# Attention and a Fourier mix on one core: score tiles in a fixed uneven order of two cycles, and the Fourier targets added on GpSimd

## The chip, the cores and the metric

The kernel runs on one core of one Trainium2 chip. A core has a matrix engine (TensorE; PE in the profile, with PEld for its weight loads), VectorE (DVE), ScalarE (ACT), GpSimd (POOL) and SyncE (SP), which only issues DMAs here. The metric is the device time of one execution in microseconds (us), lower is better.

## The reference

The input is x, 2048 tokens of 640 numbers. Two branches are computed from it and mixed by a gate per token:

```
g = sigmoid((x * gate_w).sum(-1))
a = softmax(q k^T / sqrt(20)) v, 32 heads of 20, then @ wo        # attention
b = Cr @ (x @ Hr) - Ci @ (x @ Hi)                                 # Fourier mix
out = g * a + (1 - g) * b
```

Cr, Ci are the 2048x2048 cosine and sine matrices along the sequence, Hr, Hi the 640x640 ones along the hidden axis. All inputs are given as arguments and all arithmetic is float32.

## The kernel before

**Precision.** Where float32 accuracy is wanted from the faster `fp32r` matmul, an operand is split in two (`split`, L90: a rounded copy and the remainder) and three products are added.

**Scores.** Two heads lie in the two halves of the partitions (rows 0 to 63 and 64 to 127), so a score matmul (60 or 62 rows, 128x512 results, one PSUM bank) uses one half of the array, and two on different halves run side by side. A softmax needs the row maximum first, so each score tile is computed twice. A *maximum tile* (`s_mm`, L151) is a 128x512 matmul whose maximum over 512 columns VectorE takes (L153). 41 steps (`LEAD`) later the *exponential tile* (L638) computes the same scores transposed, with minus the maximum as two more rows of the operand, and ScalarE writes the exponentials into a tile `p` (L641). A unit is a pair of heads and half of the queries: 32 steps, each of two exponential and two maximum tiles. There are 32 units (`NU`), 1024 steps. After a unit's last maximum tile, VectorE reduces the maxima once more (L159), PE transposes them (`max_chain`, L179) and SP stores them as rows of `qst`.

**Banks.** All score tiles, and that transpose, take the five banks `ps0` to `ps4` in turn (`bank`, L104). So a score matmul has to wait until the tile five places earlier has been read by its reader, ScalarE or VectorE. PE executes in program order: an instruction that waits holds back everything behind it.

**Cycles.** Four steps make a cycle. At its end comes the burst: `av_step` (L429) multiplies the exponentials of eight finished tiles by v, 16 matmuls on L435, into the bank `av`. So a cycle has eight exponential tiles, eight maximum tiles and one burst, 256 cycles in all.

**Fillers.** Between score tiles PE gets pieces of the Fourier branch, called fills here: a fill is two 320-column matmuls, one on each half of the array. In the first 54 cycles they come from `hid_tile` (L287, x times the hidden DFT, 15 fills a cycle, one tile each cycle); after three cycles without, they come from `dft_step` (L510), 48 for each of 56 units of the sequence DFT. A DFT unit is spread over three cycles (16 fills each, 26 units) or four (12 fills each, 30 units). In a cycle they stand in seven slots, after each pair of score tiles but the last (`goals`, `fill`). A step's order on PE is: exponential, maximum, fills, exponential, maximum, fills.

**The targets.** The sequence DFT is done with sums and differences of its blocks (`PRODUCTS`), so that each product is added to one or two targets, tiles of y. At a unit's end ScalarE and VectorE read its two banks into `m` (L529, L530), and `finish_y` (L537) works it into each target on VectorE: for the first product of a target `y = m * gs` (L544, 32 times), for a later one `y = m * gs + y` (L542, 64 times) with y loaded from memory before. gs is (1 - g) or -(1 - g), a column for each token tile (`ngate`). The target is stored by SP three steps later.

**GpSimd** prepares the DFT's operands: the sum or difference of two blocks (L406, L420) and their split (L94, L95), normalises o (L467), and issues loads of `kst` and `qst`.

**The output stage** (from L683): for each of 16 token tiles, y is loaded, the attention output is multiplied by wo (30 matmuls on L98 to L100 in two half tiles, each in one of the five banks) and VectorE adds `ps * gate + y` (L701). In VectorE's queue the split of the o of tile tt + 2 (`fins`, L95) stands behind tile tt's two additions. The last unit's normalisation (`rest`) runs here too: its DMAs are issued by GpSimd, `store_l` and `load_l` before the first tile, the others after tiles 2 to 4.

Of the kernel before, what the change touches and what calls it, by code (L numbers as in the profile page):

```python
# [10 lines left out]
F32 = mybir.dt.float32  # L11
R = mybir.dt.float32r
AF = mybir.ActivationFunctionType
ALU = mybir.AluOpType
# [4 lines left out]
P = 128  # L19
# [3 lines left out]
DH = 20  # L23
ND = D // P
NS = S // P
NP = H // 2
HE = D // 2
VW = 2 * (DH + 1)
KROWS = 3 * DH
NU = 2 * NP  # L30
BW = HE + 2
LEAD = 41
HEAD = 10

# [21 lines left out]
def mix_kernel(ctx: ExitStack, tc: tile.TileContext, xa, wqk, wb, cdft, wo, out):  # L56
# [7 lines left out]
    const = pools(name="const", bufs=1)  # L64
# [20 lines left out]
        pool.memset(f32(t), 1.0)  # L85
    logit = const.tile([P, NS], F32, name="logit")
    gate = const.tile([P, NS], F32, name="gate")
    ngate = {g: const.tile([P, NS], F32, name=f"ngate{g + 1}") for g in (1, -1)}

    def split(dst1, dst2, src, e1, e2):  # L90
        if e1 is act:
# [12 lines left out]
    def bank():  # L104
        return ps_w.tile([P, 512], F32, name=f"ps{next(turn) % 5}")

    def pair_tile():
        return work.tile([P, 2, 512], F32, name="p", bufs=5)
# [10 lines left out]
    def load_stack(p):  # L119
        kt, qt = kst[p % 2], qst[p % 2]  # L120
        u = S // 2
        for t, o, two, one, cs in ((kt, D, 0, 2, slice(0, S)), (qt, 0, 1, 0, slice(0, u)), (qt, 0, 1, 0, slice(u, S))):
            for h in range(2):
                r = (2 * p + h) * DH
                b = 64 * h
                rows = slice(o + r, o + r + DH)
                yield f32(t[b + two * DH : b + (two + 2) * DH, cs]), qk_scr[:, rows, cs]
                yield f32(t[b + one * DH : b + (one + 1) * DH, cs]), qk_scr[0, rows, cs]

    def q_unit(n):  # L130
        u = n % 2 * (S // 2)
        return qst[n // 2 % 2][:, u : u + S // 2]
# [4 lines left out]
    def at_step(i, fn):  # L137
        later.setdefault(i, []).append(fn)


    def s_mm(i, h):
        n, s = divmod(i, 32)
        if n >= NU:
            return lambda: None
        qt, kc = divmod(s, 4)
        q, k = q_unit(n), kst[(n // 2) % 2]
        if n not in mx:
            mx[n] = small.tile([P, 2, 8, 4], F32, name="mx", bufs=2)
        ps = bank()
        b = 64 * h  # L150
        pe.matmul(ps, q[b : b + KROWS, qt * P : (qt + 1) * P],  # L151
                  k[b : b + KROWS, kc * 512 : (kc + 1) * 512], start=True, stop=True)
        return lambda: dve.tensor_reduce(mx[n][:, h, qt, kc : kc + 1], ps, axis=AX.X, op=ALU.max)  # L153

    def s_end(i):
        n, s = divmod(i, 32)
        if n < NU and s == 31:
            nms[n] = small.tile([P, 16], F32, name="nm", bufs=2)
            dve.tensor_reduce(nms[n], mx.pop(n).rearrange("p h q c -> p (h q) c"), axis=AX.X, op=ALU.max, negate=True)  # L159
        if s == 1 and 0 < n <= NU:  # L160
            max_chain(n - 1)
# [77 lines left out]
    def flush(keep=0):  # L239
        while len(stores) > keep:  # L240
            sp.dma_start(*stores.pop(0))
# [133 lines left out]
    act.activation(gate, logit, AF.Exp, scale=-1.0)  # L375
    dve.tensor_scalar(gate, gate, 1.0, None, op0=ALU.add)
    dve.reciprocal(gate, gate)
    for g in (1, -1):
        dve.tensor_scalar(ngate[g], gate, float(-g), float(g), op0=ALU.mult, op1=ALU.add)


    at = {}
# [46 lines left out]
    def av_step(i, n, kt):  # L429
        v = vts[n // 2]  # L430
        pp = [pts.pop((n, kt, qc)) for qc in range(2)]
        for qc in range(2):
            for h in range(2):
                j = 2 * qc + h
                pe.matmul(av[32 * j : 32 * j + DH + 1, :], v[:, kt, h * (DH + 1) : (h + 1) * (DH + 1)],  # L435
                          pp[qc][:, h, :], start=kt == 0, stop=kt == NS - 1)
        if kt == NS - 1:
            unit_end(i, n)
# [98 lines left out]
    def finish_y(target, t, m, y):  # L537
        sg, th, hf = target
        tt = th * HT + t
        gs = ngate[sg][:, tt : tt + 1]  # L540
        if (tt, hf) in seen:
            dve.scalar_tensor_tensor(y, m, gs, y, op0=ALU.mult, op1=ALU.add)  # L542
        else:
            dve.tensor_scalar(y, m, gs, None, op0=ALU.mult)  # L544
        seen.add((tt, hf))
        at_step(now[0] + 3, functools.partial(sp.dma_start, y_scr[tt, :, hf * HE : (hf + 1) * HE], y))

# [2 lines left out]
    def run_extras(g, most):  # L550
        while extras and most and extras[0][0] <= now[0]:
            extras.pop(0)[1]()
            most -= 1
        if more(g):
            n = g // (HT * NS) + 1
            preps.append(load_a(n, made.setdefault(n, 0)))
            made[n] += 1
        if len(preps) > 2 or preps and not more(g):
            preps.pop(0)()
# [8 lines left out]
    def start_dft():  # L568
        flush()
        proj.release()  # L570
        apool.append(pools(name="apool", bufs=1))
# [14 lines left out]
    done = 0  # L586
# [16 lines left out]
    cycles += [(edge[u], edge[u + 1], 3 * NS) for u in range(UNITS)]  # L603
    at_goal = 0
    for c0, c1, count in cycles:
        slots = [(4 * c + k, z) for c in range(c0, c1) for k in (1, 2, 3, 4) for z in range(2 - k // 4)]
        for f, slot in enumerate(slots):
            goals[slot] = at_goal + count * (f + 1) // len(slots)
        at_goal += count

    def fill(i, z):
        nonlocal done
        while done < goals.get((i, z), 0):
            next(fills)
            done += 1

    for i in range(total + 1):
        now[0] = i
        n, s = divmod(i, 32)
        for fn in later.pop(i, ()):  # L620
            fn()
        if s % 2 == 0:
            flush()
        if i < total:
            kt, qc = divmod(s, 2)
            if s == 0 and n % 2 == 0:
                p = n // 2
                if p + 1 < NP:
                    at_step(i + 6, functools.partial(load_v, p + 1))
                    for j, args in enumerate(load_stack(p + 1)):  # L630
                        at_step(i + 2 + 2 * j, functools.partial(pool.dma_start, *args))
            q, k = q_unit(n), kst[(n // 2) % 2]
            pp = pts[n, kt, qc] = pair_tile()

            def mixed(h):
                b = 64 * h
                pt = bank()
                pe.matmul(pt, k[b : b + KROWS + 2, kt * P : (kt + 1) * P],  # L638
                          q[b : b + KROWS + 2, qc * 512 : (qc + 1) * 512], start=True, stop=True)
                most = s_mm(i + LEAD, 1 - h)  # L640
                act.activation(pp[:, h], pt, AF.Exp, scale=float(DH) ** -0.5)  # L641
                most()

            mixed(0)
            fill(i, 0)
            mixed(1)
            s_end(i + LEAD)
        if start + 2 <= i < start + 2 + HT:
            for k in range(2):
                at_step(i + 3, load_a(0, 2 * (i - start - 2) + k))  # L650
        if i and i % 4 == 0:
            run_extras(max(done - HIDS, 0) // 3, 2)
            j = i // 2 - 2
            for kt in (j, j + 1):
                av_step(i, kt // NS, kt % NS)
        else:
            fill(i, 1)
        if i % 4 == 2:
            c = i // 4
            if c + HEAD in (NS, 2 * NS):  # L660
                load_wb(3 + (c + HEAD) // NS, pool, pool)()
            if c in (HID - 5, HID - 3):
                load_c((c - HID + 5) // 2)()
            if c == HID + 1:
                cfin.append(load_c(2))
        if i == start:
            start_dft()
        if total - 10 <= i < total - 4 and i % 2 == 0:
            tt = (i - total + 10) // 2
            fins[tt] = load_o(tt)  # L670
        if i == total - 3:
            fins[0]()
    assert done == at_goal
    now[0] = total + 4
    run_extras(2 * NS * UNITS, 99)
# [7 lines left out]
    def load_y(tt):  # L683
        ys[tt] = pair_tile().rearrange("p z c -> p (z c)")[:, :D]
        sp.dma_start(ys[tt], y_scr[tt])

    flush()
    for tt in range(4):
        load_y(tt)
    for fn in rest[:2]:  # L690
        fn()
    fins[1]()
    for tt in range(NS):
        y, o = ys.pop(tt), ops.pop(tt)
        for hf in range(2):
            ps = bank()[:, :HE]
            for d in range(ND):
                w = wos[d, hf]
                three(ps, o[:, 0, d], o[:, 1, d], w[:, 0], w[:, 1], d == 0, d == ND - 1)
            ye = y[:, hf * HE : (hf + 1) * HE]  # L700
            dve.scalar_tensor_tensor(ye, ps, gate[:, tt : tt + 1], ye, op0=ALU.mult, op1=ALU.add)  # L701
        if 0 < tt < NS - 3:
            load_y(tt + 3)
        for fn in {2: rest[2:5], 3: rest[5:6], 4: rest[6:]}.get(tt, ()):
            fn()
        if tt + 3 < NS:
            fins[tt + 3] = load_o(tt + 3)
        sp.dma_start(out[tt * P : (tt + 1) * P, :], y)
        if tt + 2 < NS:
            fins[tt + 2]()  # L710


# [33 lines left out]
```

## Time and profile before

| | us |
|---|---|
| median of 3 runs | 2012.11 (2010.03 to 2013.65) |
| profiled execution, time | 2012.72 |
| profiled execution, span of its instructions | 2011.0 |
| first burst begins, last burst ends its unit | 281.8, about 1936 |
| mean granted TensorE clock | 0.997 |

The loop over the 256 cycles takes 1650 of the 2011 us; before it lie the projections, after it 75 us of output stage. The start of a burst (the first of 16 matmuls on L435) marks a cycle in the timeline. From burst to burst most cycles take 6.29 us where they have 12 fills, 6.46 with 15 and 6.59 with 16. 112 of the 120 cycles with 12 fills have maxima; the last eight have none left (the maxima run 41 steps ahead) and take 4.75 us. A unit's last maxima and their transpose lengthen one cycle in eight, by 0.33 us with 12 fills and by 0.2 us with 15 or 16.

An engine's busy share is an average over all stages, and a PE that is "busy" may be streaming slowly: matmul durations overlap, so starts are what to read.

### The profile page before, as it was taken

The numbers are of one execution on the slowest core, as the hardware profiler recorded it, in microseconds if no ns is written. First come the engines' busy times: TensorE is split into PE (matmuls) and PEld (weight loads), VectorE is DVE, ScalarE is ACT, GpSimd is POOL, SyncE is SP. The second block draws the span as 40 slices with busy tenths as digits, with TensorE's granted clock in tenths as the row PEclk, the third lists the DMA queues.
The fourth block names the chain that finished last, engine by engine and source line by source line (L and its number), as shares of the span: only waits on it lengthen the run. The fifth ranks groups of instructions, "written<-read, shape, count | busy, mean of one in ns | idle before, by whom it ended". The sixth has DMA issues, their size and how long they took to land. (4 is left out here: it accounts for less than half of the span.)

```text
span 2011.0 us, 44080 instructions
## 1 busy us (share of the span) xinstructions
PE 1974.8 (98%) x17080; PEld 1397.7 (70%) x17080; DVE 1501.9 (75%) x2516; ACT 1253.3 (62%) x2337; POOL 986.6 (49%) x898
## 2 busy tenths in 40 slices
PE   8999999999999999999999999999999999999999
PEld 7987767666675666666666666666666666666679
DVE  3144568878887888888888888888888888888423
ACT  4221147777776666677666666766766676667751
POOL 1210001111006888556368876974775689576510
PEclk9999999999999999999999999999999999999999
DMA  6653321313125475435266736563555556444345
GB/s 218 168 166 132 128 90 45 83 50 82 35 60 161 143 204 159 118 100 153 93 169 194 207 133 194 175 184 100 165 149 145 163 171 200 131 149 144 95 150 184
DMA packets 196514, 281.05 MB, mean 140 GB/s; under 512 B 73372, under 2 KB 137916, under 8 KB 194384
## 3 DMA queue, kind: packets, MB, share of 16 engines
q1 hardware_dynamic: 158992, 246.20, 39.6%
q0 software_dynamic: 37312, 32.03, 6.4%
q8 instruction: 134, 2.20, 0.5%
q14 instruction: 76, 0.62, 0.1%
HBM read 213.81 MB, written 63.70 MB: 138 GB/s over the span
## 5 line engine op out<-in xcount | busy, mean ns | idle before, releaser
L153 DVE TENSOR_REDUCE mx<-ps 128x1 f32<-128x512 f32 x2048 | 1262.2, 683 | 233.8 <-PE ps L151 230.1
L641 ACT ACTIVATE p<-ps 128x512 f32<-128x512 f32 x2048 | 1122.6, 598 | 446.0 <-PE ps L151 354.6
L151 PE MATMUL ps<-kst,qst 60*128 60x512 f32 x2048 | 926.1, 460 | 8.0 <-ACT p L641 3.7
L638 PE MATMUL ps<-qst,kst 62*128 62x512 f32 x2048 | 823.9, 409 | 9.0 <-DVE mx L153 7.6
L510 PE MATMUL yp<-a,part 64*128 64x320 f32 x5376 | 734.0, 309 | 0.1
L510 PEld LDWEIGHTS yp<-a,part 64*128 64x128 f32 x5376 | 596.6, 187 | 23.9 <-DVE m L530 0.3
L638 PEld LDWEIGHTS ps<-qst,kst 62*128 62x128 f32 x2048 | 376.9, 185 | 235.9 <-DVE mx L153 66.9
L435 PE MATMUL av<-p,v 128*21 128x512 f32 x4096 | 494.7, 599 | 0.1
L151 PEld LDWEIGHTS ps<-kst,qst 60*128 60x128 f32 x2048 | 372.0, 184 | 59.5 <-ACT p L641 27.7
L95 POOL TENSOR_TENSOR part<-raw,part 128x1024 fp32r<-128x1024 f32 x112 | 267.1, 2385 | 9.0
L435 PEld LDWEIGHTS av<-p,v 128*21 128x21 f32 x4096 | 98.8, 100 | 226.8 <-issue 219.8
L287 PE MATMUL yp<-wb,xs 64*128 64x320 f32 x1920 | 238.1, 308 | 0.4 <-ACT raw L295 0.3
L94 POOL CAST part<-raw 128x1024 fp32r<-128x1024 f32 x112 | 116.8, 1043 | 205.2 <-PE yp L510 198.6
L406 POOL TENSOR_TENSOR raw<-raw,raw 128x1024 f32<-128x1024 f32 x78 | 188.3, 2414 | 50.1 <-DMA raw<-in_cdft 39.6
L287 PEld LDWEIGHTS yp<-wb,xs 64*128 64x128 f32 x1920 | 205.7, 187 | 9.1 <-ACT raw L295 0.6
L467 POOL TENSOR_TENSOR o<-o,rb 128x512 f32<-128x512 f32 x32 | 41.6, 1300 | 160.7 <-DMA rb<-r_scr 130.0
L94 POOL CAST wb<-raw 128x966 fp32r<-128x966 f32 (+1 forms) x4 | 3.4, 856 | 229.7 <-PE av L435 195.5
L95 POOL TENSOR_TENSOR a<-araw,a 128x320 fp32r<-128x320 f32 x112 | 98.1, 876 | 9.0
L95 DVE TENSOR_TENSOR p<-ps,p 128x512 fp32r<-128x512 f32 x40 | 27.5, 691 | 94.2 <-ACT p L92 94.2
L98 PE MATMUL ps<-xs,part 128*128 128x512 f32 x200 | 80.7, 403 | 9.1 <-ACT xs L92 7.5
L92 ACT ACTIVATE p<-ps 128x512 fp32r<-128x512 f32 x40 | 23.7, 597 | 101.5 <-PE ps L100 101.5
L420 POOL TENSOR_TENSOR araw<-araw 128x320 f32<-128x320 f32 x80 | 71.4, 892 | 20.4 <-DMA araw<-a_scr 19.9
(67 smaller groups left out, 1339.0 us busy)
## 6 DMA issues: line engine op xcount, KB each, us to landing
raw<-in_cdft SPq DMA_DIRECT2D x192, 512.0 KB
araw<-a_scr SPq DMA_DIRECT2D x192, 160.0 KB
qk_scr<-p SPq DMA_DIRECT2D x40, 512.0 KB
y_scr<-yt SPq DMA_DIRECT2D x96, 160.0 KB
kst<-qk_scr POOLq DMA_DIRECT2D x32, 320.0 KB, 12.2
qst<-qk_scr POOLq DMA_DIRECT2D x64, 160.0 KB, 8.8
a_scr<-raw SPq DMA_DIRECT2D x64, 160.0 KB
yt<-y_scr SPq DMA_DIRECT2D x64, 160.0 KB
```

What stands on the lines that cost most here:

```text
L94: e1.tensor_copy(dst1, src)
L95: e2.tensor_tensor(dst2, src, f32(dst1), op=ALU.subtract)
L98: pe.matmul(ps, st1, mv1, start=first, stop=False)
L151: pe.matmul(ps, q[b : b + KROWS, qt * P : (qt + 1) * P], k[b : b + KROWS, kc * 512 : (kc + 1) * 512], start=True, stop=True)
L153: return lambda: dve.tensor_reduce(mx[n][:, h, qt, kc : kc + 1], ps, axis=AX.X, op=ALU.max)
L287: pe.matmul(yp[h][:, :HE], xs[r, xz, d, cs], w[r, wz, d, :HE], start=d == 0 and z == 0, stop=d == ND - 1 and z == 2)
L406: pool.tensor_tensor(raws[0], raws[0], raws[1], op=ALU.add if PRODUCTS[n][0][1][0] > 0 else ALU.subtract)
L420: pool.tensor_tensor(raws[0], raws[0], raws[1], op=ALU.add if PRODUCTS[n][1][1][0] > 0 else ALU.subtract)
L435: pe.matmul(av[32 * j : 32 * j + DH + 1, :], v[:, kt, h * (DH + 1) : (h + 1) * (DH + 1)], pp[qc][:, h, :], start=kt == 0, stop=kt == NS - 1)
L510: pe.matmul(yp[h][:, :HE], c[r, cz, cs], a[r, az], start=s == 0 and z == 0, stop=s == NS - 1 and z == 2)
L638: pe.matmul(pt, k[b : b + KROWS + 2, kt * P : (kt + 1) * P], q[b : b + KROWS + 2, qc * 512 : (qc + 1) * 512], start=True, stop=True)
L641: act.activation(pp[:, h], pt, AF.Exp, scale=float(DH) ** -0.5)
```

## The change

There are two independent parts.

**The order.** The loop over steps becomes a loop over cycles that follows a string of letters, one string for even cycles and one for odd: e is an exponential tile, m a maximum tile, F a place for fills, B the burst. `FIRST` gives which half of the array (head) each step's first tile of a kind uses. An even cycle has 8 e, 7 m and 11 places, an odd one 8 e, 9 m and 17 places. The number of fills of a cycle stays 12, 15 or 16, for even and odd cycles alike, and is spread evenly over the cycle's places. What went with a step (`later`, loads, `flush`) is put in `begin` and `end`, the burst in `burst`.

**The targets.** `finish_y` goes to GpSimd, without the gate: `y = y + m` or `y - m`, or `y = m * sg` for a first product. The factor (1 - g) is multiplied in at the output stage, by GpSimd, once for each token tile (`scale_y`, 128x640): tiles 0 and 1 after the first two steps of `rest`, tile tt + 2 at the end of tile tt, behind that tile's step of `rest`. VectorE's two additions of a tile wait for it.

```
+ORDER = ("emmeFFFFmeFFemFFmeFFemFeemB", "ememmFFFFFeFmFemFFFeeFFmmFFFFFeemmB")
+FIRST = {"e": (1, 1, 1, 0, 0, 1, 1, 0), "m": (0, 0, 0, 0, 0, 0, 0, 1)}
...
-    for g in (1, -1):
-        dve.tensor_scalar(ngate[g], gate, float(-g), float(g), op0=ALU.mult, op1=ALU.add)
+    dve.tensor_scalar(ngate, gate, -1.0, 1.0, op0=ALU.mult, op1=ALU.add)
...
-            dve.scalar_tensor_tensor(y, m, gs, y, op0=ALU.mult, op1=ALU.add)
+            pool.tensor_tensor(y, y, m, op=ALU.add if sg > 0 else ALU.subtract)
         else:
-            dve.tensor_scalar(y, m, gs, None, op0=ALU.mult)
+            pool.tensor_scalar(y, m, float(sg), None, op0=ALU.mult)
...
+            share = count * (c + 1 - c0) // (c1 - c0) - count * (c - c0) // (c1 - c0)
+            places = ORDER[c % 2].count("F")
+            goals[c] = [at_goal + share * (f + 1) // places for f in range(places)]
...
+    def score(kind):
+        x = heads[kind]
+        heads[kind] += 1
+        i, z = divmod(x, 2)
+        h = z ^ FIRST[kind][(i - (LEAD if kind == "m" else 0) - 1) % 8]
+        if kind == "m":
+            s_mm(i, h)()
+            if z:
+                s_end(i)
+            return
...
+    for kind in "emme":
+        score(kind)
+    for c in range(total // 4):
+        for kind in ORDER[c % 2]:
+            if kind == "F":
+                fill(c)
+            elif kind == "B":
+                burst(c)
+            else:
+                score(kind)
...
+    def scale_y(tt):
+        pool.tensor_scalar(ys[tt], ys[tt], ngate[:, tt : tt + 1], None, op0=ALU.mult)
...
     for fn in rest[:2]:
         fn()
     fins[1]()
+    for tt in range(2):
+        scale_y(tt)
...
         if tt + 2 < NS:
+            scale_y(tt + 2)
             fins[tt + 2]()
```

More of the change, by code (lines that the diff above doesn't have):

```diff
@@ L87, in mix_kernel @@
     gate = const.tile([P, NS], F32, name="gate")
-    ngate = {g: const.tile([P, NS], F32, name=f"ngate{g + 1}") for g in (1, -1)}
+    ngate = const.tile([P, NS], F32, name="ngate")
     def split(dst1, dst2, src, e1, e2):
@@ L539, in finish_y @@
         tt = th * HT + t
-        gs = ngate[sg][:, tt : tt + 1]
         if (tt, hf) in seen:
-            dve.scalar_tensor_tensor(y, m, gs, y, op0=ALU.mult, op1=ALU.add)
+            pool.tensor_tensor(y, y, m, op=ALU.add if sg > 0 else ALU.subtract)
         else:
-            dve.tensor_scalar(y, m, gs, None, op0=ALU.mult)
+            pool.tensor_scalar(y, m, float(sg), None, op0=ALU.mult)
         seen.add((tt, hf))
@@ L605, in mix_kernel, with fill, begin @@
     for c0, c1, count in cycles:
[L606 to L611, printed above, removed]
+        for c in range(c0, c1):
+            share = count * (c + 1 - c0) // (c1 - c0) - count * (c - c0) // (c1 - c0)
+            places = ORDER[c % 2].count("F")
+            goals[c] = [at_goal + share * (f + 1) // places for f in range(places)]
+            at_goal += share
+    def fill(c):
         nonlocal done
-        while done < goals.get((i, z), 0):
+        goal = goals[c].pop(0) if c in goals else 0
+        while done < goal:
             next(fills)
             done += 1
-    for i in range(total + 1):
+    def begin(i):
         now[0] = i
@@ L623, in mix_kernel, with end @@
             flush()
-        if i < total:
[L625 to L647, printed above, removed]
+        if s == 0 and n % 2 == 0:
+            p = n // 2
+            if p + 1 < NP:
+                at_step(i + 6, functools.partial(load_v, p + 1))
+                for j, args in enumerate(load_stack(p + 1)):
+                    at_step(i + 2 + 2 * j, functools.partial(pool.dma_start, *args))
+        if i < total:
+            pts[n, s // 2, s % 2] = pair_tile()
+    def end(i):
         if start + 2 <= i < start + 2 + HT:
@@ L650, in mix_kernel @@
                 at_step(i + 3, load_a(0, 2 * (i - start - 2) + k))
[L651 to L657, printed above, removed]
         if i % 4 == 2:
@@ L665, in mix_kernel @@
                 cfin.append(load_c(2))
-        if i == start:
-            start_dft()
         if total - 10 <= i < total - 4 and i % 2 == 0:
@@ L672, in mix_kernel, with burst @@
             fins[0]()
+    heads = {"e": 0, "m": 2 * LEAD}
+    def score(kind):
[8 more added lines that the diff above has]
+            return
+        if z == 0 and i <= total:
+            begin(i)
+        if i < total:
+            n, s = divmod(i, 32)
+            kt, qc = divmod(s, 2)
+            q, k = q_unit(n), kst[(n // 2) % 2]
+            b = 64 * h
+            pt = bank()
+            pe.matmul(pt, k[b : b + KROWS + 2, kt * P : (kt + 1) * P],
+                      q[b : b + KROWS + 2, qc * 512 : (qc + 1) * 512], start=True, stop=True)
+            act.activation(pts[n, kt, qc][:, h], pt, AF.Exp, scale=float(DH) ** -0.5)
+            if z:
+                end(i)
+    def burst(c):
+        run_extras(max(done - HIDS, 0) // 3, 2)
+        for kt in (2 * c, 2 * c + 1):
+            av_step(now[0], kt // NS, kt % NS)
+        if c == HID - 1:
+            start_dft()
+    for kind in "emme":
[8 more added lines that the diff above has]
+                score(kind)
     assert done == at_goal
```

## The prediction

> **What bounds the kernel now.** I read the page's busy times and groups first, then the chain of waits, then the timeline of single cycles. The page:
>
> ```profile
> PE 1974.8 (98%) x17080; PEld 1397.7 (70%) x17080; DVE 1501.9 (75%) x2516; ACT 1253.3 (62%) x2337; POOL 986.6 (49%) x898
> ...
> L153 DVE TENSOR_REDUCE mx<-ps 128x1 f32<-128x512 f32 x2048 | 1262.2, 683 | 233.8 <-PE ps L151 230.1
> L641 ACT ACTIVATE p<-ps 128x512 f32<-128x512 f32 x2048 | 1122.6, 598 | 446.0 <-PE ps L151 354.6
> L151 PE MATMUL ps<-kst,qst 60*128 60x512 f32 x2048 | 926.1, 460 | 8.0 <-ACT p L641 3.7
> L638 PE MATMUL ps<-qst,kst 62*128 62x512 f32 x2048 | 823.9, 409 | 9.0 <-DVE mx L153 7.6
> ```
>
> No other engine is near PE. But an undisturbed score matmul shows 0.39 us, and the means here are 0.41 and 0.46: some start late and without their weights. Who waits for whom:
>
> ```profile
> ACT p L641 <- PE ps L151: 354.6, 227, 3.2
> DVE mx L153 <- PE ps L151: 230.1, 224, 3.1
> ...
> PEld ps L638 <- DVE mx L153: 66.9, 87, 1.5
> ...
> PEld ps L151 <- ACT p L641: 27.7, 111, 3.3
> ```
>
> The readers wait some 225 times, about once a cycle: they run dry during the burst. PE waits for them in turn, at banks. One cycle with 16 fills (start, length, engine, group):
>
> ```profile
> 1000.84 0.50 PE L638 MATMUL ps<-qst,kst 62*128 62x512 f32 x1
> ...
> 1001.37 4.11 ACT L641 ACTIVATE p<-ps 128x512 f32<-128x512 f32 x7 [1.65 <-PE ps L151]
> 1001.40 5.01 DVE L153 TENSOR_REDUCE mx<-ps 128x1 f32<-128x512 f32 x8 [0.58 <-PE ps L151]
> ...
> 1005.58 1.91 PE L435 MATMUL av<-p,v 128*21 128x512 f32 x16
> ...
> 1007.42 0.18 PEld L638 LDWEIGHTS ps<-qst,kst 62*128 62x128 f32 x1 [0.85 <-DVE yt L542]
> ```
>
> From such starts come the steps for walking an order by hand. On its half of the array a score holds 0.235 us, a fill 0.147. From the last score to the burst 0.33, from the burst to the next score 1.84. After the burst the first reads begin 0.57 after their matmuls. VectorE's reads follow each other every 0.60 (eight in 5.01) and end 0.685 after they start. A score that waited starts 0.055 after the read that frees its bank; its weights are not there yet, so it takes 0.49 instead of 0.39: its reader starts 0.57 after it, its half is held 0.10 longer. ScalarE can follow every 0.49 and is nowhere last. Walking the old order so gives 6.31 us with 12 fills (the timeline has 6.29) and 6.62 with 16 (6.59): good to 0.03.
>
> **The order.** Number the score tiles of a cycle; tile k needs the bank of tile k - 5.
>
> *Odd cycle* (e m e m m ... m m B, nine maxima). Reads of tiles 2, 4, 5, 7 start at 0.57, 1.17, 1.77, 2.37 after the cycle's first score; 7's ends at 3.05. Tile 12 needs that bank: matmul 3.11, read 3.68 to 4.36. Tile 17, the last, needs 12's: 4.42, burst at 4.42 + 0.43 = 4.85, next cycle at 6.69. This is VectorE's chain, so 12, 15 or 16 fills make no difference (PE's load is at most 4.8).
>
> *Even cycle* (seven maxima). Reads of 2 and 3 at 0.57 and 1.17, ending 1.85; tile 8 at 1.91, read at 2.48; 9's read 3.08 to 3.76; tile 14 at 3.82, burst at 4.25, next cycle at 6.09. With 15 fills 6.10. With 16, PE's load is last (0.33 + 7 x 0.235 + 16 x 0.147 + 0.09 = 4.42, less some overlap): 6.25.
>
> Against two old cycles: 12 fills 12.78 for 12.58, +0.20; 15 fills 12.79 for 12.92, -0.13; 16 fills 12.94 for 13.18, -0.24. Over 56, 26.5 and 39 pairs: +11.2 - 3.4 - 9.4 = -1.6 us.
>
> One more bank is needed in one cycle of eight, for the transpose of a unit's maxima (L179). By the step count it now comes behind odd tile 17 and takes tile 13's bank. With L159 (0.22 us and its gap) ahead of them, 12 and 13 are read late: 13's read ends at 5.11, the transpose starts at 5.16, the burst 0.21 later at 5.37: 0.52 later than without. The old order paid 0.33 (12 fills) or 0.2, 0.27 on average. 31 x 0.25 = +7.8.
>
> The order's bounds: below, PE's load alone. The cycles without maxima take 4.75 with 12 fills; four scores more on each half make 5.69, the ninth on one half in every odd cycle 5.81: 112 x 0.48, and by the same sum 53 x 0.21 and 78 x 0.19, -80 us. Above, even cycles as long as odd ones: 112 x 0.40 + 53 x 0.23 + 78 x 0.10, +65. I take the walk, since it repeats the old cycles to 0.03; that error alone is 255 x 0.03, 8 us either way.
>
> What hung on a step (loads, stores, the burst) is issued at the same step as before, the same DMAs in the same order on SP and GpSimd; a step is 1.6 us, and a shift by one would be covered by the leads given below. Nothing is added for it.
>
> **The targets.** L542 and L544 (least, median, longest in ns) and the worst place:
>
> ```profile
> L542 DVE SCALAR_TENSOR_TENSOR yt<-m,ngate,yt x64: 529/550/2671, 865.2 to 1934.1; 128x320 f32<-128x320 f32 x64
> ```
> ```profile
> L544 DVE TENSOR_SCALAR yt<-m,ngate x32: 366/412/2531, 680.0 to 1210.9; 128x320 f32<-128x320 f32 x32
> ```
> ```profile
> 1098.50 2.65 POOL L406 TENSOR_TENSOR raw<-raw,raw 128x1024 f32<-128x1024 f32 x1
> 1098.81 2.53 DVE L544 TENSOR_SCALAR yt<-m,ngate 128x320 f32<-128x320 f32 x1
> ...
> 1101.99 0.18 PEld L638 LDWEIGHTS ps<-qst,kst 62*128 62x128 f32 x1 [1.31 <-DVE mx L153]
> ```
>
> Beside a GpSimd operation VectorE's stretches until GpSimd's ends; the maxima behind it are late and PE stands 1.3 us. Where nothing collides, the 0.4 and 0.55 lie in VectorE's idle time at the burst and cost nothing: cycles with two of them take the usual 6.29 and 6.59. Nine cycles with stretched ones exceed theirs by 10 us together, the transposes' share taken off. Moved, they leave VectorE with reads of PSUM and L530 (468/492/493 ns, never stretched). Bounds: 0 to the whole stretch, 64 x (922 - 550) + 32 x (796 - 412) = 36 us; I take the 10, which is PE's own loss.
>
> GpSimd gets 64 additions of 0.89 (L420, same size), 32 multiplications of about 0.47 (L94 on 128x320) and 16 of about 0.7 (between L94's 0.47 and 1.04 for 128x1024): 83 us. It is busy 872 of the 1233 us of the DFT, in its fullest 20 us stretches 19 of 20. Yet each operand is ready 14 to 24 us before PE's first use of it, 8.5 at the least, so an addition of 0.9 ahead of it is hidden; with that lead gone each would cost its 0.9.
>
> The Trainium skill (GPSIMD Engine Reference, 4.1 Engine selection) says to use VectorE for elementwise work, GpSimd being about twice as slow on two inputs. The rows have 0.89 for 0.55, 1.6 times; by the page's 2 GpSimd would carry 64 x 0.2, 13 us, more, and the sum would stay, as neither lies on PE's path.
>
> **The output stage.** `scale_y(0)` and `(1)` stand on GpSimd behind `load_l`, which waits for the stores of l to land:
>
> ```profile
> 1937.25 2.00 POOL L451 DMA_DIRECT2D l_scr<-o  x4 [28.85 <-ACT o L442]
> 1944.00 0.58 POOL L454 DMA_DIRECT2D lc<-l_scr  x1 [4.74 <-DVE p L701]
> ```
>
> So y of tile 0 is scaled at 1945.4 instead of used at 1938.7. Five banks hold 2.5 tiles (4.4 us each), until 1947.2, but VectorE's split for tile 2 (0.82) stands behind tile 0's two additions (0.55 each): done at 1947.3, while PE, which began at 1936.2, wants it at 1945.0. +2.4 us. Tiles 4 and 5, scaled behind `load_r` and the normalisation, come up to 3 us late, which banks and the splits' lead of a tile cover. Bounds 0 (the stores land sooner) and 5 (the next tiles late as well).
>
> **Sum.** -1.6 + 7.8 - 10 + 2.4 = -1.4. The profiled execution's span of 2011.0 becomes 2009.6, its time of 2012.7 becomes 2011.3; the median lies 0.6 under it: 2010.7, rounded to 2011. No change, as far as a measurement can tell (0.2%, 4 us).
>
> **Rivals.**
> *Faster: a waiting score's weights are loaded ahead.* Then tiles 8, 14, 12 and 17 cost 0.1 less each, 0.2 a cycle over 241: 2011 - 48 = 1963. Against it, scores that wait now show 0.49; for it, fills get theirs in time on the same half (0.147 apart, weight loads of 0.187).
> *Slower: the odd cycle's rest runs into the next.* At its burst VectorE still has 13, 16 and 17 to read, until 6.27, and at a unit's end L530 (0.49): 6.76, while the next first read is due at 6.69 + 0.57 = 7.26. From 0.5 us late on, it delays the even chain one for one: at 0.7 late 0.2 a pair, 127 pairs, 2036. Only the transposes' cycles (0.55 more on VectorE) come near.
> *Slower: GpSimd late, and SP behind it.* A second target stands behind a block's preparation (2.4 + 1.0 + 2.4); SP's store of it, due three steps later, waits, and behind it the rows of maxima. These have 9.6 us to use, their four issues and landing take 5. From 4.6 us late on PE stops; 1 us at each of 31 units is 2042. Against: the leads above.
> *The targets' stalls were no loss* (PE would have stopped there for another bank): 2021.
>
> **How the numbers follow.** The forecast has 0.45, from 2003 to 2019: 0.16 of it under 2007, 0.18 within 4 us, 0.11 over 2015. Faster by the weights, or by less stalling of that kind, 0.20; VectorE's rest 0.17, GpSimd 0.10, stalls no loss 0.08. So faster 0.36, same 0.18, slower 0.46. The range from 1975 (leaving out the lower half of the faster case) to 2040.
>
> **What would show it.** Cycles of two lengths by turns, near 6.1 or 6.25 and 6.7; in the odd ones PE waiting for VectorE at tiles 12 and 17; VectorE idle over 1 us after an even burst only; no L153 beside a stretched operation; the first output addition near 1945. It is wrong if even cycles with 12 fills are not 0.2 under the old, if the odd ones are under 6.6, or if PE waits for GpSimd's operands.

## The result: slower by 0.28%

| | median, us | lowest to highest | runs |
|---|---|---|---|
| before | 2011.62 | 2008.16 to 2016.22 | 15 |
| after | 2018.11 | 2012.52 to 2023.24 | 15 |

The ratio is 1.0028 (95% interval 1.0017 to 1.0039), 5.6 us. The forecast was no change, -1.4 us, with 0.46 on slower. Four lines of the page after, then three waits after and, last, one before (engine and line that waited, who released it: us in total, times, longest):

```profile
PE 1979.6 (98%) x17080; PEld 1373.5 (68%) x17080; DVE 1451.6 (72%) x2419; ACT 1244.9 (62%) x2337; POOL 1097.1 (54%) x1010
...
L160 DVE TENSOR_REDUCE mx<-ps 128x1 f32<-128x512 f32 x2048 | 1288.5, 683 | 274.2 <-PE ps L158 253.6
L680 ACT ACTIVATE p<-ps 128x512 f32<-128x512 f32 x2048 | 1113.7, 598 | 461.4 <-PE ps L158 288.4
L158 PE MATMUL ps<-kst,qst 60*128 60x512 f32 x2048 | 722.4, 437 | 9.0 <-DVE mx L160 2.9
```
```profile
POOL yt L547 <- DVE m L536: 169.9, 30, 17.3
...
POOL yt L549 <- DVE m L536: 80.5, 12, 12.2
...
POOL part L101 <- PE yp L516: 17.5, 6, 5.1
```
```profile
POOL part L94 <- PE yp L510: 198.6, 52, 9.3
```

VectorE is 50 us less busy and GpSimd 110 us more, as the moved work wants; PE is still at 98%. GpSimd now stands for 250 us at a target's operation (L547, L549) until the product `m` is there. Most of this is not additional idle time: before, it stood 199 us at a split (L94) until PE's fills were done with its buffer, and 17.5 us of that are left. What is new is that it goes on only when `m` has been made, at the burst, and has the target to do first.

The start of each burst shows where the time went. The loop from the first to the last but one burst (the last one, 3.5 us later, is counted with what comes after) is split into what its cycles take by the median of their kind and what single cycles take above that:

| profiled execution, us | first burst | loop | of it medians | of it excess | after the loop | span |
|---|---|---|---|---|---|---|
| before | 281.8 | 1647.3 | 1627.7 | 16.9 | 81.9 | 2011.0 |
| after | 280.8 | 1651.0 | 1629.2 | 18.4 | 86.7 | 2018.6 |

(Excess is what a cycle takes beyond 0.12 us over its median; what lies under that is the small rest.) The cycles as such cost 1.5 us more. The excess looks unchanged, but it is another excess: the cycles that a stretched target lengthened, some 10 us, are gone, and in their place stand a few long stalls: 6.4 us at 750, 3.1 us at 1151, and two that were there before and are longer, by 2.4 us at 430 and by 1.3 us at 624. These two lie ahead of the first target (674.8), and kernels of the old order, alike up to there, differ among themselves by as much: at 430 from 3.1 us (before) to 4.6 (e11), at 624 from 1.3 (before) to 2.9 (e10). So only the stalls at 750 and 1151 can be put down to the targets. The output stage costs 4.8 us more.

**The cycles.** Burst starts in the timeline after (start, length, engine, group), and below them the weight loads that begin after a wait in the two cycles from 951.69 (in brackets the idle time before, and what ended it):

```profile
951.69 1.92 PE L441 MATMUL av<-p,v 128*21 128x512 f32 x16
...
957.75 1.91 PE L441 MATMUL av<-p,v 128*21 128x512 f32 x16
...
964.41 1.92 PE L441 MATMUL av<-p,v 128*21 128x512 f32 x16
```
```profile
955.45 0.18 PEld L158 LDWEIGHTS ps<-kst,qst 60*128 60x128 f32 x1 [0.18 <-DVE mx L160]
...
957.32 0.18 PEld L678 LDWEIGHTS ps<-qst,kst 62*128 62x128 f32 x1 [0.22 <-DVE mx L160]
...
959.59 0.18 PEld L678 LDWEIGHTS ps<-qst,kst 62*128 62x128 f32 x1 [0.85 <-issue]
...
962.70 0.19 PEld L158 LDWEIGHTS ps<-kst,qst 60*128 60x128 f32 x2 [0.22 <-DVE mx L160]
...
963.92 0.24 PEld L158 LDWEIGHTS ps<-kst,qst 60*128 60x128 f32 x2 [0.25 <-ACT p L680]
```

6.06 us for the even cycle, 6.66 for the odd one. The waits stand where the walk put them. Even cycle, first score at 953.53: tile 8 forecast 1.91 later (955.44), tile 14 3.82 later (957.35). Odd cycle, first score at 959.59: tile 12 3.11 later (962.70), tile 17 4.42 later (964.01; it is the second of the two loads that the last line joins, at 963.98).

**The longest stall**, in the timeline of all engines:

```profile
751.38 1.28 POOL L473 TENSOR_TENSOR o<-o,rb 128x512 f32<-128x512 f32 x1
...
752.68 1.68 SPq L481 DMA_DIRECT2D o_scr<-o  x4
...
756.37 0.60 ACT L448 ACTIVATE o<-av 128x512 f32<-128x512 f32 x1 [5.21 <-DMA o_scr<-o]
...
757.50 0.79 PE L678 MATMUL ps<-qst,kst 62*128 62x512 f32 x1 [3.75 <-ACT p L680]
```

GpSimd normalises `o` at 751.38 (before: 747.8). Only then can SP store it, and the store has to land before ScalarE may copy the next `av` into `o`, which has one buffer. ScalarE stands 5.21 us at that copy, the exponentials behind it are not read, and PE stands 3.75 us for their banks. What follows is a second price (stretch, length, busy time of PE, PEld, DVE, ACT, POOL, granted clock, DMA share, GB/s):

```profile
740.00:750.00 10.00, 10.00 (x102) 7.67 (x98) 8.88 (x15) 7.69 (x15) 9.57 (x11) 1.00 0.40 116
757.00:763.90 6.90, 6.40 (x40) 5.15 (x44) 2.76 (x4) 4.42 (x8) 6.69 (x6) 0.52 0.82 281
```

For 6.8 us, from about 757 on, PE is granted half its clock. GpSimd is busy 9.57 of the 10 us before it: there was no idle time to catch up in.

### The profile page after: what moved, and what is told of

It is laid out like the page before. It is cut to its first block, busy times and chain, and to the rows that moved or that the text cites. A ratio compares the mean times of both kernels' runs of the same rounds, so it can differ in the third digit from the quotient of the medians.

```text
span 2018.6 us, 43894 instructions
## 1 busy us (share of the span) xinstructions
PE 1979.6 (98%) x17080; PEld 1373.5 (68%) x17080; DVE 1451.6 (72%) x2419; ACT 1244.9 (62%) x2337; POOL 1097.1 (54%) x1010
## 5 line engine op out<-in xcount | busy, mean ns | idle before, releaser
L160 DVE TENSOR_REDUCE mx<-ps 128x1 f32<-128x512 f32 x2048 | 1288.5, 683 | 274.2 <-PE ps L158 253.6
L158 PE MATMUL ps<-kst,qst 60*128 60x512 f32 x2048 | 722.4, 437 | 9.0 <-DVE mx L160 2.9
L678 PE MATMUL ps<-qst,kst 62*128 62x512 f32 x2048 | 713.8, 432 | 9.0 <-ACT p L680 8.0
L516 PE MATMUL yp<-a,part 64*128 64x320 f32 x5376 | 658.4, 310 | 0.1
L516 PEld LDWEIGHTS yp<-a,part 64*128 64x128 f32 x5376 | 573.3, 187 | 21.0 <-DVE m L536 0.3
L678 PEld LDWEIGHTS ps<-qst,kst 62*128 62x128 f32 x2048 | 318.1, 185 | 268.7 <-issue 137.2
L158 PEld LDWEIGHTS ps<-kst,qst 60*128 60x128 f32 x2048 | 330.2, 185 | 60.7 <-DVE mx L160 28.5
L294 PE MATMUL yp<-wb,xs 64*128 64x320 f32 x1920 | 221.7, 313 | 0.1
L547 POOL TENSOR_TENSOR yt<-yt,m 128x320 f32<-128x320 f32 x64 | 56.1, 876 | 170.0 <-DVE m L536 169.9
L101 POOL CAST part<-raw 128x1024 fp32r<-128x1024 f32 x112 | 116.4, 1040 | 25.2 <-PE yp L516 17.5
```

The lines of the kernel that those rows point to most:

```text
L101: e1.tensor_copy(dst1, src)
L158: pe.matmul(ps, q[b : b + KROWS, qt * P : (qt + 1) * P], k[b : b + KROWS, kc * 512 : (kc + 1) * 512], start=True, stop=True)
L294: pe.matmul(yp[h][:, :HE], xs[r, xz, d, cs], w[r, wz, d, :HE], start=d == 0 and z == 0, stop=d == ND - 1 and z == 2)
L516: pe.matmul(yp[h][:, :HE], c[r, cz, cs], a[r, az], start=s == 0 and z == 0, stop=s == NS - 1 and z == 2)
L547: pool.tensor_tensor(y, y, m, op=ALU.add if sg > 0 else ALU.subtract)
L678: pe.matmul(pt, k[b : b + KROWS + 2, kt * P : (kt + 1) * P], q[b : b + KROWS + 2, qc * 512 : (qc + 1) * 512], start=True, stop=True)
```

## The experiments

Each ratio is to the kernel before, run by turns with it on the same chip. The kernel before had medians of 2013.16 (e1 to e4), 2012.64 (e5 to e8) and 2013.74 (e9 to e11).

| kernel | us | ratio | 95% | first burst | loop | medians | excess | stage |
|---|---|---|---|---|---|---|---|---|
| after | 2018.11 | 1.0028 | 1.0017-1.0039 | 280.8 | 1651.0 | 1629.2 | 18.4 | 86.7 |
| e1 order only | 2051.14 | 1.0186 | 1.0166-1.0207 | 279.4 | 1688.1 | 1637.5 | 47.9 | 81.9 |
| e2 targets only | 1997.56 | 0.9930 | 0.9917-0.9943 | 275.8 | 1635.2 | 1627.4 | 6.5 | 84.1 |
| e3 scaling on ScalarE | 2016.13 | 1.0016 | 1.0006-1.0027 | 278.3 | 1653.7 | 1631.2 | 19.3 | 81.9 |
| e4 targets a burst later | 2009.53 | 0.9984 | 0.9974-0.9994 | 283.1 | 1639.0 | 1629.5 | 6.4 | 85.8 |
| e5 two buffers for o | 2003.60 | 0.9959 | 0.9942-0.9975 | 279.2 | 1637.9 | 1629.8 | 5.5 | 84.3 |
| e6 new order, all three | 2002.18 | 0.9947 | 0.9931-0.9963 | 280.4 | 1637.2 | 1632.0 | 3.0 | 82.3 |
| e7 old order, all three | 1993.89 | 0.9912 | 0.9892-0.9931 | 277.5 | 1631.6 | 1625.6 | 5.7 | 81.9 |
| e8 uneven order in places | 1987.15 | 0.9873 | 0.9853-0.9893 | 276.8 | 1623.9 | 1620.4 | 5.6 | 82.1 |
| e9 e1, next burst | 2021.07 | 1.0039 | 1.0026-1.0052 | 281.8 | 1660.4 | 1632.8 | 22.9 | 81.9 |
| e10 before, same burst | 2031.28 | 1.0084 | 1.0063-1.0106 | 278.3 | 1673.2 | 1632.2 | 38.5 | 81.9 |
| e11 e2, same burst | 2008.31 | 0.9973 | 0.9961-0.9984 | 279.9 | 1643.1 | 1624.6 | 16.3 | 84.5 |

(The columns from "first burst" on are of one profiled execution each. The first burst comes between 275.8 and 283.1 in kernels whose code up to there is nearly the same, so a single span is uncertain by some us; the loop and its parts are the better witnesses.)

**e1: the order alone, the targets on VectorE as before.**

```
-            pool.tensor_tensor(y, y, m, op=ALU.add if sg > 0 else ALU.subtract)
+            dve.scalar_tensor_tensor(y, m, gs, y, op0=ALU.mult, op1=ALU.add)
...
-            pool.tensor_scalar(y, m, float(sg), None, op0=ALU.mult)
+            dve.tensor_scalar(y, m, gs, None, op0=ALU.mult)
...
-            scale_y(tt + 2)
```

> The new order alone, the targets on VectorE and the gate as before. Theory A (GpSimd stands waiting for m in its queue, so its later work comes late): this kernel has none of that. The loop gains and loses what the cycles' medians say, +2.6 us, and keeps the old 10 us of stretched target operations: about 2014 for 2011.6, ratio 1.001, output stage as before (75 us). Theory B (the order itself makes the new long stalls): 2018 or more, ratio 1.003, with stalls of 2 to 6 us in the loop as in the changed kernel.

38 us slower than before, far from every expected number. The targets' two lines (number, then least, median and longest in ns):

```profile
L549 DVE SCALAR_TENSOR_TENSOR yt<-m,ngate,yt x64: 529/1200/2856, 864.1 to 1970.0; 128x320 f32<-128x320 f32 x64
```
```profile
L551 DVE TENSOR_SCALAR yt<-m,ngate x32: 365/872/1853, 672.1 to 1220.8; 128x320 f32<-128x320 f32 x32
```

The medians were 550 and 412 before, with the same tiles. The lengthened cycles say it too: with a target of usual length they take their usual time to 0.04 us, with a stretched one some 0.6 (even) and 0.9 us (odd) more at the median, about 46 us in all. So in the new order more targets run beside an operation of GpSimd. They also run later: a target in the burst that reads its unit starts 1.8 us after the burst's start, behind VectorE's reading of the unit (median), and a stretched one ends at 3.4; before they start at 1.0 and end at 2.5. The next cycle's first reads are due at about 2.4, so a stretch that mostly cost nothing before now delays them. Why shows in their place: they start under 3 us after their unit's `m` 56 times of 96, before 3 times. A unit's products are read at the burst after its last fill, and `finish_y` is given the step `now[0] + 1`. In the old order the last fill comes in the cycle's last step, 4c + 4; the targets are due at 4c + 5 and wait for the next burst. The new order ends a cycle's fills one exponential earlier (two are left behind them instead of one), in step 4c + 3; the targets are due at 4c + 4, and the first of them runs in the same burst (two such pieces a burst, the reading and one target), at the moment when the unit's end lets GpSimd go on. This became theory C, for e9 to e11.

**e2: the targets alone, with the old order.**

```
-            dve.scalar_tensor_tensor(y, m, gs, y, op0=ALU.mult, op1=ALU.add)
+            pool.tensor_tensor(y, y, m, op=ALU.add if sg > 0 else ALU.subtract)
...
+            scale_y(tt + 2)
```

> The old order with the targets on GpSimd and the factor at the output. Theory A: -10 us for the stretched operations, +4.9 in the output stage, and some +8 of late GpSimd work in the loop (the copy to o, loads of kst and qst): 2014 to 2016, ratio 1.001 to 1.002. Theory B: -10 + 4.9, 2006 or 2007, ratio 0.9975.

Also off every expected number, on the other side: 14 us faster. The excess falls by 10.4 us, what the prediction gave for the stretched targets. GpSimd waits less than half as long for `m` as in the kernel after:

```profile
POOL yt L540 <- DVE m L529: 85.3, 19, 17.6
...
POOL yt L542 <- DVE m L529: 28.5, 7, 11.2
```

The order and the targets are therefore not independent: +38 and -14 together give +5.6.

**e3: the scaling of y on ScalarE.**

```
-        pool.tensor_scalar(ys[tt], ys[tt], ngate[:, tt : tt + 1], None, op0=ALU.mult)
+        act.activation(ys[tt], ys[tt], AF.Copy, scale=ngate[:, tt : tt + 1])
```

> The changed kernel with the factor (1 - g) multiplied by ScalarE instead of GpSimd at the output. If the output stage's 4.9 us come from GpSimd's 1.89 us per tile behind load_l, the stage goes back to about 75 us and the kernel to 2013, 5 us under the changed one, with no half-clock stretch near 1951. If they come from VectorE's order behind the additions whoever scales, it stays within 2 us of 2018.

The stage is back at 81.9 us, as before the change. The first two scalings on GpSimd and the first additions after (timeline), and the same two lines in e3:

```profile
1946.65 7.47 POOL L716 TENSOR_SCALAR p<-p,ngate 128x640 f32<-128x640 f32 x4
...
1948.59 1.01 DVE L734 SCALAR_TENSOR_TENSOR p<-ps,gate,p 128x320 f32<-128x320 f32 x2 [7.27 <-POOL p L716]
```
```profile
1940.48 2.41 ACT L716 ACTIVATE p<-p,ngate 128x640 f32<-128x640 f32 x3
...
1941.77 0.55 DVE L734 SCALAR_TENSOR_TENSOR p<-ps,gate,p 128x320 f32<-128x320 f32 x1 [0.27 <-PE ps L107]
```

VectorE stands 7.27 us after, 0.27 in e3. The stage is as expected, but of its 4.8 us only 2 reached the median, where 5 were expected. In the profiled execution the loop is 2.7 us longer than after, with a stall at 1171 and half clock there; why the other executions gained no more is not known.

**e4: the targets one burst later, rest as after.**

```
-                extras.append((now[0] + 1, functools.partial(finish_y, out_, t, m, y)))
+                extras.append((now[0] + 5, functools.partial(finish_y, out_, t, m, y)))
```

> The changed kernel with each target put into GpSimd's queue one burst later, when m is there. Theory A: GpSimd's wait for m (250 us in all) goes, the normalisation and the issues of kst and qst come sooner, the stalls of 2 to 6 us in the DFT's part go: 2009 to 2011, 7 to 9 us under the changed kernel. Theory B: no change, 2018; the waits for m go without a gain.

0.44% under after, 8.9 us, as expected. The stalls at 750 and 1151 are gone, the excess is 6.4 instead of 18.4. GpSimd runs ahead of PE, so a later place in its queue is less waiting there:

```profile
POOL yt L547 <- DVE m L536: 90.8, 18, 17.3
...
POOL yt L549 <- DVE m L536: 30.2, 5, 11.6
```

(It stands 99.5 us for the fills here, 17.5 after: a part of the standing has moved back to where it was before.)

**e5: two buffers for o, rest as after.**

```
-        o = pa.tile([P, 512], F32, name="o")
+        o = pa.tile([P, 512], F32, name="o", bufs=2)
```

> The changed kernel with two buffers for o, so that the copy of a unit's attention result never waits for the store of the one before. If the stalls near 430 and 750 us (5.6 and 6.4 us in the changed kernel's profile, with a half clock after them) come from that copy, both go: about 2008 to 2010, 8 to 10 us under the changed kernel's 2018; the stall near 1151 (GpSimd's late issue of qst) stays. If the copy only happens to wait where something else is late as well, the time stays within 3 us of 2018.

0.69% under after, 14 us where 8 to 10 were expected. GpSimd waits for `m` as long as ever (167.9 and 76.7 us), but no copy waits for a store of `o`: the stalls at 430 and 750 and the half clock behind them are gone. The stretches shown above for after, now in e5:

```profile
740.00:750.00 10.00, 10.00 (x105) 7.74 (x103) 8.46 (x14) 7.31 (x14) 9.71 (x8) 1.00 0.28 72
757.00:763.90 6.90, 6.90 (x67) 4.27 (x67) 6.25 (x12) 5.00 (x11) 6.61 (x8) 1.00 0.77 246
```

GpSimd is as full as before, PE never stands, the clock stays at 1.00. So at 750 GpSimd's lateness reached PE through the one buffer of `o`. The stall that was expected to stay, at 1151, is there (at 1145), but PE stands 0.93 us instead of 1.58 and the clock is not halved. Not all of the 14 us is the change's: the stall at 430 is in the kernel before too.

**e6 and e7: late targets, ScalarE's scaling and two o together, in the new order (e6) and in the old (e7).**

```
+                extras.append((now[0] + 5, functools.partial(finish_y, out_, t, m, y)))
...
+        act.activation(ys[tt], ys[tt], AF.Copy, scale=ngate[:, tt : tt + 1])
...
+        o = pa.tile([P, 512], F32, name="o", bufs=2)
```

> The changed kernel with all three: targets one burst later, the factor on ScalarE, two buffers for o. What is left of the difference to the kernel before is then the order itself: 2009.5 of the late targets, less 4.8 in the output stage, less 4 to 5 for the stall near 430: about 2000.

> The same three on the old order with the targets on GpSimd: 1997.6 less 2.3 in the output stage, less 3.3 near 425 us, the late targets giving nothing more as no stall of theirs is left: about 1992. Against the new order so mended it shows the order's own price: +2.6 us by the cycles' medians (my walk had +6); if the order has another cost, 10 us or more.

With most other stalls gone in both, the new order costs 8.3 us by the medians of the runs, 5.6 by the loops and 6.4 by the sums of usual cycles, between the two expected numbers; the walk had +7.8 - 1.6 = +6.2. The pair is not wholly clean: in the old order, + 5 puts the targets two bursts after the reading, in the new order one. GpSimd's waits for `m` are 22 us in e7 and 122 in e6.

**e8: the uneven order only where the walk gives it a gain:** pairs of cycles with 16 fills in both, or 12 and then 16, without a transpose, 29 of 127 pairs; the others in the old order; the three mends as in e7.

```
+PLAIN = "emFemFemFemFemFemFemFemB"
...
+        uneven[p] = p % 4 != 2 and shares.get(2 * p, 0) in (12, 16) and shares.get(2 * p + 1) == 16
+    def letters(c):
+        return ORDER[c % 2] if uneven[c // 2] else PLAIN
```

> The same, with the uneven order only in pairs of cycles of the DFT where its medians are under the old ones: both with 16 fills, or 12 and then 16, and no transpose; 29 of 127 pairs. By the medians 6.7 us under the old order mended, about 1985. If the order's gain with 16 fills needs its neighbours to be uneven too, no change against that kernel.

6.7 us under e7, 1.27% under before: the fastest of all. No half clock is left in the loop, as the mean granted clock says (after: 0.993):

```profile
core 0: 1982.7 us, clock 0.999
```

**e9, e10, e11: the targets' burst alone.** e9 is e1 with the targets in the next burst; e10 is before, and e11 is e2, with the targets in the same burst.

```
e9   -                extras.append((now[0] + 1, functools.partial(finish_y, out_, t, m, y)))
e9   +                extras.append((now[0] + 2, functools.partial(finish_y, out_, t, m, y)))
e10, e11  -           extras.append((now[0] + 1, functools.partial(finish_y, out_, t, m, y)))
e10, e11  +           extras.append((now[0], functools.partial(finish_y, out_, t, m, y)))
```

> The new order alone, targets on VectorE, but each unit's first target put off to the burst after the one that reads the unit, where it stood before. Theory C: the new order ends a cycle's fills two exponentials earlier, so the first target slips into the reading burst by itself, beside GpSimd's operations that the unit's end releases; 62 of 96 target operations are stretched in the order alone, 41 in the kernel before. Put off, the time falls from 2051 to 2013 to 2018, and few targets start within 3 us of m. Theory D (the order leaves VectorE no room for targets at any burst): 2040 or more.

> The kernel before, with one thing changed: the first target of a unit in the burst that reads it. Theory C: the stretched operations come here too, 15 to 40 us over 2012.6 (in the old order VectorE has a little more room at each burst). Theory D: no change, 2011 to 2015.

> The old order with the targets on GpSimd, the first target of a unit in the burst that reads it. Theory C: GpSimd waits for m as in the changed kernel (about 250 us in all, against 114 at the next burst), its later work slips, and the copy to o and the first maxima on new kst and qst wait: 5 to 12 us over 1997.6. Theory D, or a lateness that needs the new order: within 3 us of 1997.6.

The line of the later targets in e9, in e10:

```profile
L549 DVE SCALAR_TENSOR_TENSOR yt<-m,ngate,yt x64: 530/610/2679, 868.3 to 1947.2; 128x320 f32<-128x320 f32 x64
```
```profile
L542 DVE SCALAR_TENSOR_TENSOR yt<-m,ngate,yt x64: 532/1322/3116, 863.0 to 1954.2; 128x320 f32<-128x320 f32 x64
```

(The fills end one exponential earlier, not two as the expectation says.) e9 takes back 30.7 of e1's 38 us, and 40 targets are stretched instead of 62 (before: 41). It ends over the expected 2013 to 2018: the 7.3 us that are left are the order's, with 5.1 in the sum of usual cycles and 6 in excess in the profiled execution, which was the slowest of the nine. e10 adds 17.5 us to the kernel before with nothing else changed, by the same sign: a median of 1322 ns. e11 adds 0.43%, 8.7 us, to e2, and its waits are those of the kernel after:

```profile
POOL yt L540 <- DVE m L529: 163.9, 30, 17.6
...
POOL yt L542 <- DVE m L529: 75.6, 11, 11.4
```
```profile
ACT o L441 <- DMA o_scr<-o: 13.5, 4, 4.2
```

ScalarE waits four times for a store of `o`, 13.5 us in all; in e2 it was once, 4.2 us.

So the place of one call, which the order's letters shift by one step, costs 17 to 31 us with the targets on VectorE and about 9 with them on GpSimd.

## Why the prediction was wrong

**The order's cycles: right.** Odd cycles 6.66 us (forecast 6.69), even ones 6.06, 6.16 and 6.26 with 12, 15 and 16 fills (6.09, 6.10, 6.25), the transpose behind tile 17 +0.54 (+0.52). The sum was +6.2. The sums of usual cycles of kernels that differ in the order alone are apart by 2.1 (e2 and e4), 4.6 (e11 and after) and 5.1 us (before and e9); those of the old order spread by 3 us among themselves, so no more can be had from them. One item the walk left out: every fourth odd cycle, the one in which VectorE computes a unit's reciprocals (0.24 us), takes 6.76 us, with nothing lost there in the old order. That is 0.10 us some 30 times, 3 us.

**What hung on a step: wrong, and this is the step that failed.** The prediction had "issued at the same step as before ... Nothing is added for it", and looked only at loads, stores and the burst. `finish_y` hangs on a step too, by `now[0] + 1`, and the one exponential more that the new order has behind the last F makes it due in the same burst. e4 measures this step in the kernel after: 8.9 us; e11 in the kernel with the targets alone: 8.7.

**GpSimd: hidden at the operands, as forecast, and not elsewhere.** No wait of PE for an operand that GpSimd prepared is in the trace after. But GpSimd works in order, and I priced only its operands' leads, not what else stands in its queue: the normalisation of `o` and the loads of `kst` and `qst`. SP's wait for the normalisation before it can store `o` shows it, before and after:

```profile
SPq L475 <- POOL o L467: 15.4, 3, 9.4
```
```profile
SPq L481 <- POOL o L473: 35.8, 12, 9.6
```

The rival "GpSimd late, and SP behind it" was right in kind and named the wrong store: not that of the targets with the rows of maxima behind it, but that of `o` with ScalarE behind it. At 1151 it is a load: GpSimd issues it at 1153.60, loads of `qst` take 5.1 to 9.5 us to land there, and PE resumes with a maximum tile at 1158.87. This last link I read from the times; no run changed it alone. (The profile puts that wait down to ScalarE, which had long been done.) It fits that e5, where the load is issued at the same place in the cycle, keeps the stall.

**The targets' stalls: right.** -10 forecast, -10.4 in e2's excess. As a whole e2 gained 14 us, more than the -10 + 2.4 that the prediction has for the targets; of the rest, 6 us lie before the first burst of the profiled execution and are not explained.

**The output stage: the sum right, its term wrong, and a price missed.** A scaling takes 1.89 us, not the 0.7 assumed between L94's 0.47 and 1.04. By the prediction's own steps that makes 3.4 instead of 2.4. Three runs with GpSimd's scaling (e2, e5, e11) show +2.2 to +2.6, e4 +3.9 and the kernel after +4.8. After, the clock went to half for 3.4 us at 1951 (1.7 us lost), after PE had stood 2.0 us for the split; in e2 it stood 1.34, because l's stores landed 0.67 us sooner (GpSimd's wait for them is 3.32 there, 3.99 after).

**An account.** Three steps lead from before to after, one change at a time: e2 moves the targets, e11 puts them in the reading burst, after has the new order besides. By their ratios these cost -14.1, +8.7 and +11.1 us, together the measured +5.6; each is uncertain by some 3 us. The forecast had -10 + 2.4 = -7.6, nothing, and -1.6 + 7.8 = +6.2. So the step priced at nothing is the largest miss. The targets gave 6.5 us more than forecast and the order cost 4.9 more, and it is luck that these two nearly cancel. (e2 to e4, with the targets in the next burst, has +10.9 for the order, before to e9 +7.3 by the medians.)

**Other rivals.** "The targets' stalls were no loss" falls with e2. "The odd cycle's rest runs into the next" isn't seen: in e1, with VectorE's queue longer by the targets, cycles with targets of usual length are over by 0.04 us at most. "Weights loaded ahead" isn't either: waiting scores still start as the walk has them.

## What to carry to other kernels

When a change reorders a loop, list everything that is scheduled by a step number or "at the next such point", also what is far from the edit, and see on which side of its point each falls afterwards: here one step cost 9 us with the targets on GpSimd and up to 31 with them on VectorE. Work given to an engine that executes in order costs what stands behind it in the queue, and single buffers downstream turn that lateness into stalls: a second buffer for `o` was worth 14 us and the cheapest mend, in part because it also took away a stall that was there before. Price a stall of PE at more than its length, for the clock may be halved after it.

## What the runs showed of the hardware

**Half clock after short gaps.** One-us stretches of the kernel after around its stall at 1157 (columns as above):

```profile
1157.00:1158.00 1.00, 0.29 (x2) 0.00 (x0) 0.97 (x3) 0.95 (x2) 1.00 (x2) 1.00 0.52 123
1158.00:1159.00 1.00, 0.13 (x2) 0.16 (x4) 0.19 (x1) 0.00 (x0) 1.00 (x3) 1.00 0.79 164
1159.00:1160.00 1.00, 1.00 (x12) 1.00 (x14) 0.62 (x1) 0.00 (x0) 0.94 (x2) 0.77 1.15 266
1160.00:1161.00 1.00, 1.00 (x7) 0.54 (x4) 0.07 (x1) 0.43 (x1) 0.92 (x2) 0.50 0.96 344
...
1163.00:1164.00 1.00, 1.00 (x12) 0.11 (x4) 0.48 (x2) 0.00 (x0) 1.00 (x1) 1.00 0.32 90
```

PE stood 1.58 us; about half a microsecond after it resumed the clock was halved for 3.4 us. Gaps of 2.0 us (in the stage) and 3.75 us (at 754) were followed by 3.4 and 6.8 us. But the length of the gap does not decide: these two, the first from the kernel before, the second from the one after, were followed by no half clock at all.

```profile
437.56 0.50 PE L151 MATMUL ps<-kst,qst 60*128 60x512 f32 x1 [2.92 <-ACT p L641]
```
```profile
631.85 0.47 PE L158 MATMUL ps<-kst,qst 60*128 60x512 f32 x1 [2.15 <-DMA qst<-qk_scr]
```

The kernel before has 3.4 us of half clock twice, from 637 and from 651, with no gap over 0.4 us in the 7 us ahead of either; that is in and right behind the three cycles without fills. The Trainium skill (TensorE: Matmul & The Clock Gate, Part 1) states half clock after at least one idle window of about 3.4 us. The length of the slow stretches, once and twice 3.4, agrees with such a window; the gaps of 1.58 and 2.0 were shorter than it, and so was every gap ahead of 637 and 651. What decides is left open.

**GpSimd's prices.** The multiplication by a constant (L549) is dearer than the two-input addition (L547), and with a factor per token on twice the columns (L716) it takes nearly twice as long again:

```profile
L549 POOL TENSOR_SCALAR yt<-m x32: 999/1009/1056, 674.8 to 1209.7; 128x320 f32<-128x320 f32 x32
```
```profile
L547 POOL TENSOR_TENSOR yt<-yt,m x64: 857/874/917, 863.7 to 1934.6; 128x320 f32<-128x320 f32 x64
```
```profile
L716 POOL TENSOR_SCALAR p<-p,ngate x16: 1872/1887/1898, 1946.7 to 2001.0; 128x640 f32<-128x640 f32 x16
```

I had taken 0.47 for the first, from the cast of the same size. ScalarE does the last in 0.83 us (median in e3).
